# Stage two of a spectral block with its first products turned round: kf as weights, halves swapped by transfers, no second transposes

## The chip, the cores and the metric

One kernel runs on one core of a Trainium2 chip. The core has a matrix engine (PE, with its weight loads shown apart as PEld), a vector engine (DVE), an activation engine (ACT), a general engine (POOL) and a sync engine (SP) that here only issues transfers. Sixteen transfer engines (DMA) move data between the chip's main memory and the core's SBUF, whose 128 partitions the engines work on; PE writes into banks of PSUM, each of 128 partitions by 512 floats. The metric is the time of one execution on the device in microseconds, as the median of the runs.

## The reference: what is computed

```python
x = A_x                                    # [1, 2048, 512], float32
mod = (silu(c) @ w_mod).reshape(1, 6, 1, 512)
sa, ca, ga, sb, cb, gb = ...               # the six rows of mod
h = layernorm(x) * (1 + ca) + sa
X = rfft2(h, axes=(-2, -1)) * (w_r + 1j * w_i)      # w: [2048, 257]
x = x + ga * irfft2(X, s=(2048, 512))
h = layernorm(x) * (1 + cb) + sb
a = h @ w1 + b1                            # [2048, 1376]
x = x + gb * ((a * tanh(softplus(a))) @ w2)
```

A two-dimensional real Fourier transform of the normed input is multiplied, frequency by frequency, with a complex weight and transformed back. Then follow a second norm and a dense layer pair with the Mish function.

## The kernel before

The kernel has four stages, each with its order of work written out by hand (`manual_schedule`), so that on every engine and on every transfer queue instructions run in the order of the program text.

**Stage one** (to about 49 us) takes the 2048 rows as 128 x 16 and transforms along the 512 columns and along the 128. The result stands in `a_sb`, a tile [128, 64, 16, 8]: partition = one of 128 row frequencies, then 64 column frequencies `q`, 16 remaining rows `n`, and 8 entries (real and imaginary part of four column residues).

**Stage two** (the part that changes) does the remaining transform of length 16 x 4, the multiplication with the complex weight, and its inverse. It works on `groups` of four values of `q`, 512 columns wide: 17 groups, of which group 0 (`q` = 0) is special and has functions of its own (`z_in`, `z_mul`, `z_prod`, `z_back`, `z_out`). They are taken in the order `seq`. For a group five functions run:

- `p2_in` (L460): PE transposes the 128 x 128 blocks of `a_sb` of the group into a bank (L467), ACT copies it out (L470), and POOL adds a shift to one column per block (`p2_shift`, L478). Now the 128 lanes (16 x 4 x 2) stand on partitions.
- `p2_mul` (L480): four products (L488), with a block of the group as weights and the constant `kf` as moving data. That turns the block round again: the row frequencies stand on partitions, the lanes lie along the bank.
- `p2_prod` (L492): the complex multiplication. DVE makes two products of the bank with the real and with the imaginary weight (L504). Since real and imaginary lanes lie beside each other along the row, the sums of the crossed halves (L509, L510) are plain additions, on POOL except for five groups, whose first half DVE takes. The weight of a group is a tile of 256 KB; the first eight lie in `wqa`, the others in `wqb`, and all are loaded by SP's queue, before or at the start of the stage.
- `p2_back` (L513): PE transposes the result (L521), ACT copies it out (L524).
- `p2_out` (L527): four products with the constant `kv` (L534), and `store_d`, four ACT instructions that spread the bank over the tiles `d` (L387, L388).

A software pipeline runs these: eight `p2_in` ahead (`LEAD`), then the loop over steps `s`, where a step does `p2_prod` of group `s`, `p2_mul` of `s + 1`, `p2_in` of `s + 3`, `p2_back` of `s - 2` and `p2_out` of `s - 3`. Beside this, the steps hold the modulation columns: `mod_fetch` has SP load a 256 KB piece of `w_mod` two steps ahead into one of four buffers, and `mod_late` lets DVE multiply it with the silu row `scb` (in SBUF) and sum it up (L115). 16 such columns lie in steps 3 to 16. `flat` and `spread` write the gate out to memory and read it back to all partitions, on ACT's queue, `mod_gate` (L556) multiplies it into `kiv`, and the constants `kc` of stage three are loaded by SP in steps 13 and 15.

**Stage three** (L657 to L676) transforms back along 128 and 512 and adds to `x`. It needs all groups' `d`. **Stage four** is the dense pair. Both are dense on PE until the end.

PSUM has eight banks, two for each of the tags A, B, C and D: in stage two A takes `p2_in`, B `p2_mul`, C `p2_back`, D `p2_out`. Buffers with the tags g1, g2, y, t and h exist twice each.

Of the kernel before, what the change touches and what calls it, by code (L numbers as in the profile page):

```python
# [7 lines left out]
F32 = mybir.dt.float32  # L8
# [24 lines left out]
def tile_spectral_block(ctx: ExitStack, tc: tile.TileContext, x_d, w1_d, b1_d, w2_d,  # L33
# [54 lines left out]
    saz = base.tile([P, NQ], F32, name="saz")  # L88
    mraw = big.tile([P, N2, 256], F32, name="mraw", tag="da")
# [6 lines left out]
    wqa = pw.tile([P, 8, 2, 64, 4], F32, name="wqa")  # L96
# [17 lines left out]
    def mod_column(w, out, by, waste):  # L114
        nc.vector.scalar_tensor_tensor(waste, w, by, scb, op0=ALU.mult, op1=ALU.mult, accum_out=out)  # L115
# [70 lines left out]
    def load_rest():  # L186
        nc.sync.dma_start(kf, kf_d)
        nc.sync.dma_start(wz, wz_d)
        for i in range(8):
            nc.sync.dma_start(wqa[:, i], wq_d[i])  # L190
            if i == 2:
# [104 lines left out]
    with tc.manual_schedule():  # L296
# [16 lines left out]
        nc.vector.memset(eps, EPS)  # L313
        nc.vector.memset(b1n[:, NF - 1:NF], 0.0)
# [126 lines left out]
    def z_back():  # L441
        y = st.pop(("y", 0))
        pc = bank("C")
        nc.tensor.transpose(pc[:, 0:P], y[:, 0:P], ident)
        nc.tensor.transpose(pc[0:96, P:2 * P], y[:, 160:256], ident)
        t1, t2 = buf("t"), buf("t")
# [33 lines left out]
    def p2_mul(g):  # L480
        if g == 0:
            return z_mul()
        q0, nq = groups[g]
        w = nq * P
        z = st.pop(("z", g))
        pb = bank("B")
        for i in range(nq):
            nc.tensor.matmul(pb[:, 0:w].rearrange("p (e q) -> p e q", q=nq)[:, :, i], z[:, i * P:(i + 1) * P],  # L488
                             kf[:, 0:128], start=True, stop=True)
        st["pb", g] = pb  # L490

    def p2_prod(g):  # L492
        if g == 0:
            return z_prod()
        q0, nq = groups[g]
        w = nq * P
        pb = st.pop(("pb", g))
        pbv = pb[:, 0:w].rearrange("p (c j q) -> p c j q", q=nq, c=2)
        pr = []
        for i in range(2):  # L500
            t = buf(("g1", "g2")[i])
            tv = t[:, 0:w].rearrange("p (c j q) -> p c j q", q=nq, c=2)
            wt = (wqa, wqb)[q0 // 32][:, q0 // 4 % 8, i, :, q0 % 4:q0 % 4 + nq]
            nc.vector.tensor_tensor(tv, pbv, wt.unsqueeze(1).to_broadcast([P, 2, 64, nq]), op=ALU.mult)  # L504
            pr.append(t)
        y = buf("y")
        u = w // 2
        eng = nc.vector if g in (*seq[:3], *seq[-2:]) else nc.gpsimd
        eng.tensor_tensor(y[:, 0:u], pr[0][:, 0:u], pr[1][:, u:w], op=ALU.subtract)  # L509
        nc.gpsimd.tensor_tensor(y[:, u:w], pr[0][:, u:w], pr[1][:, 0:u], op=ALU.add)  # L510
        st["y", g] = y

    def p2_back(g):  # L513
        if g == 0:
            return z_back()
        q0, nq = groups[g]
        w = nq * P
        y = st.pop(("y", g))
        pc = bank("C")
        for i in range(nq):  # L520
            nc.tensor.transpose(pc[:, i * P:(i + 1) * P], y[:, 0:w].rearrange("p (e q) -> p e q", q=nq)[:, :, i],  # L521
                                ident)
        t = buf("t")
        nc.scalar.copy(t[:, 0:w], pc[:, 0:w])  # L524
        st["t", g] = t

    def p2_out(g):  # L527
# [3 lines left out]
        t = st.pop(("t", g))  # L531
        pd = bank("D")
        for i in range(nq):
            nc.tensor.matmul(pd[:, i * P:(i + 1) * P], t[:, i * P:(i + 1) * P], kv[:, 0:128],  # L534
# [4 lines left out]
    work_mod = {s: [] for s in range(len(seq) + 4)}  # L539
    when = (3, 4, 5, 6, 6, 7, 8, 9, 9, 10, 11, 12, 12, 13, 14, 16)  # L540
# [8 lines left out]
    def mod_late(s):  # L549
        for which, k in work_mod[s]:  # L550
            w = late.pop((which, k))
            mod_column(w, cols[:, 1, which - 1, k:k + 1] if which in (1, 2) else gcol[:, which // 3, k:k + 1], 1.0, w)
# [6 lines left out]
    wqb = pw.tile([P, 8, 2, 64, 4], F32, name="wqb", tag="half")  # L559
    with tc.manual_schedule():  # L560
        for i in range(8):
            nc.sync.dma_start(wqb[:, i], wq_d[8 + i])
        for i in range(LEAD):
# [4 lines left out]
            if i in (2, 4):  # L568
                p2_mul(seq[i // 2 - 1])
# [540 lines left out]
```

## Time and profile before

| | us |
|---|---|
| median of three runs | 392.35 |
| the three runs | 390.35, 392.35, 392.66 |
| the profiled execution | 390.15 |
| its span, first to last instruction | 388.2 |
| stage two, first transpose (L467) to first product of stage three (L663) | 49.42 to 97.55 |

| engine | busy us in the span | share |
|---|---|---|
| PE | 382.0 | 98% |
| DVE | 301.1 | 78% |
| ACT | 247.4 | 64% |
| POOL | 98.2 | 25% |

In the answers of the profile a group row reads: source line, engine, operation, output and inputs by their names in the program, shapes and count, then total busy time and the mean in ns, then idle time before it and who ended it. `buf` and `bank` are the names of all work buffers and banks. A timeline row begins with start and length in us. A product or transpose in the float type used here appears on PE as one entry for a transpose and two for a product. A transfer row has the size of one transfer and the median time from issue to landing. A row by stretches has start and end, length, busy time and instruction count for PE, PEld, DVE, ACT and POOL, the granted clock, the mean busy share of the transfer engines, and GB/s.

### The profile page before, as it was taken

The numbers are of one execution on the slowest core, as the hardware profiler recorded it, in microseconds if no ns is written. First come the engines' busy times: TensorE is split into PE (matmuls) and PEld (weight loads), VectorE is DVE, ScalarE is ACT, GpSimd is POOL, SyncE is SP. The second block draws the span as 40 slices with busy tenths as digits, with TensorE's granted clock in tenths as the row PEclk, the third lists the DMA queues.
The fourth block names the chain that finished last, engine by engine and source line by source line (L and its number), as shares of the span: only waits on it lengthen the run. The fifth ranks groups of instructions, "written<-read, shape, count | busy, mean of one in ns | idle before, by whom it ended". The sixth has DMA issues, their size and how long they took to land.

```text
span 388.2 us, 7440 instructions
## 1 busy us (share of the span) xinstructions
PE 382.0 (98%) x2769; PEld 356.3 (92%) x2769; DVE 301.1 (78%) x677; ACT 247.4 (64%) x545; POOL 98.2 (25%) x132
## 2 busy tenths in 40 slices
PE   8999999999999999999999999999999999999996
PEld 8999889999999998999998998999999999899985
DVE  2898978996399989888857866965966875987994
ACT  1798756778458638965845755664674674594751
POOL 0588637685166623300000000000000010017000
PEclk9999999999999999999999999999999999999999
DMA  7999994394052411200100100100100200113011
GB/s 270 354 320 380 296 357 114 95 292 160 26 155 77 143 49 28 57 2 0 56 0 3 54 2 0 57 0 2 55 2 0 76 0 2 48 57 115 2 56 54
DMA packets 21748, 36.98 MB, mean 95 GB/s; under 512 B 4016, under 2 KB 7184, under 8 KB 21456
## 3 DMA queue, kind: packets, MB, share of 16 engines
q1 hardware_dynamic: 20992, 35.85, 27.4%
q10 hardware_dynamic: 720, 0.66, 0.9%
q8 instruction: 22, 0.36, 0.4%
q14 instruction: 14, 0.11, 0.1%
HBM read 32.30 MB, written 4.20 MB: 94 GB/s over the span
## 4 chain that ended last, share of the span: by engine, by line
PE 89%; DVE 4%; ACT 3%; DMA 1%; issue 1%; SPq 1%; DVEq 0%; ACTq 0%
PE bank L805 24%; PE bank L752 20%; PE bank L754 10%; PE bank L208 4%; PE bank L488 4%; PE bank L534 3%; PE bank L673 3%; PE bank L253 3%; PE bank L663 3%; PE bank L664 3%; PE bank L797 2%; PE bank L818 2%; PE bank L642 2%; PE bank L467 2%; PE bank L521 1%; PE bank L255 1%
## 5 line engine op out<-in xcount | busy, mean ns | idle before, releaser
L762 ACT ACTIVATE buf<-bank,b1n 128x256 f32<-128x256 f32 (+1 forms) x88 | 40.8, 472 | 66.9 <-PE bank L754 66.5
L763 DVE TENSOR_TENSOR buf<-buf,bank 128x256 f32<-128x256 f32 (+1 forms) x88 | 35.3, 416 | 38.6 <-ACT buf L762 38.6
L715 DVE TENSOR_TENSOR al<-buf,ah 128x512 fp32r<-128x512 f32 (+2 forms) x85 | 53.5, 652 | 0.9 <-ACT ah L714 0.9
L734 POOL TENSOR_TENSOR buf<-buf,modr 128x512 f32<-128x512 f32 (+1 forms) x3 | 3.9, 1295 | 183.1 <-DVE buf L763 146.5
L752 PE MATMUL bank<-h2e,w1h 128*128 128x512 f32 (+1 forms) x176 | 48.5, 397 | 0.0
L752 PE MATMUL bank<-h2o,w1h 128*128 128x512 f32 (+1 forms) x176 | 48.3, 396 | 0.0
L714 ACT CAST ah<-buf 128x512 fp32r<-128x512 f32 (+2 forms) x85 | 43.0, 548 | 1.4 <-DVE buf L779 1.1
L779 DVE TENSOR_TENSOR buf<-buf 128x128 f32<-128x128 f32 x148 | 39.8, 310 | 3.5 <-ACT buf L769 2.2
L769 ACT ACTIVATE buf<-buf 128x512 f32<-128x512 f32 (+1 forms) x48 | 28.6, 596 | 14.7 <-DVE buf L763 14.6
L805 PE MATMUL bank<-w2a,ah 128*128 128x256 f32 x161 | 34.9, 286 | 0.0
L752 PEld LDWEIGHTS bank<-h2e,w1h 128*128 128x128 f32 (+1 forms) x176 | 30.1, 187 | 4.5
L752 PEld LDWEIGHTS bank<-h2o,w1h 128*128 128x128 f32 (+1 forms) x176 | 30.1, 187 | 4.4
L805 PE MATMUL bank<-w2b,ah 128*128 128x256 f32 x147 | 31.8, 283 | 0.0
L754 PEld LDWEIGHTS bank<-h2e,w1l 128*128 128x128 f32 (+1 forms) x176 | 26.7, 185 | 4.2
L754 PEld LDWEIGHTS bank<-h2o,w1l 128*128 128x128 f32 (+1 forms) x176 | 26.7, 185 | 4.2
L754 PE MATMUL bank<-h2e,w1l 128*128 128x256 f32 (+1 forms) x176 | 27.8, 280 | 0.0
L754 PE MATMUL bank<-h2o,w1l 128*128 128x256 f32 (+1 forms) x176 | 27.8, 280 | 0.0
L805 PEld LDWEIGHTS bank<-w2a,ah 128*128 128x128 f32 x161 | 26.7, 191 | 0.0
L663 PE MATMUL bank<-kc,d 128*128 128x128 f32 x128 | 24.8, 276 | 0.5 <-ACT d L387 0.5
L664 PE MATMUL bank<-kc,d 128*128 128x128 f32 x128 | 24.7, 275 | 0.0
L805 PEld LDWEIGHTS bank<-w2b,ah 128*128 128x128 f32 x147 | 24.6, 191 | 0.0
L122 DVE BATCH_NORM_STATS2 st<-x 128x6 f32<-128x512 f32 x32 | 22.0, 688 | 0.8 <-DMA x<-in_A_x_dram 0.4
(220 smaller groups left out, 1011.2 us busy)
## 6 DMA issues: line engine op xcount, KB each, us to landing
buf<-in_B_w_dram SPq DMA_DIRECT2D x20, 256.0 KB, 2.9
x<-in_A_x_dram SPq DMA_DIRECT2D x16, 256.0 KB, 5.1
xring<-in_x_t_dram SPq DMA_DIRECT2D x16, 256.0 KB, 5.0
wm<-in_w_mod_dram SPq DMA_DIRECT2D x16, 256.0 KB, 4.4
out_dram<-x SPq DMA_DIRECT2D x7, 512.0 KB, 2.6
mraw<-in_km_dram SPq DMA_DIRECT2D x16, 128.0 KB, 5.0
wqa<-in_w_q_dram SPq DMA_DIRECT2D x8, 256.0 KB, 4.4
wqb<-in_w_q_dram SPq DMA_DIRECT2D x8, 256.0 KB, 6.6
```

What stands on the lines that cost most here:

```text
L122: nc.vector.bn_stats(t, x[:, n, :])
L663: nc.tensor.matmul(o, dj[:, 0:128], kc[0][:, n, :], start=True, stop=False)
L664: nc.tensor.matmul(o, dj[:, 64:192], kc[1][:, n, :], start=False, stop=True)
L714: nc.scalar.copy(h, r)
L715: nc.vector.tensor_tensor(l, r, plain(h), op=ALU.subtract)
L752: nc.tensor.matmul(ps, w1h[:, k, fs], h[:, k], start=(k == 0), stop=False)
L754: nc.tensor.matmul(ps[:, 0:256], w1l[:, k, fs], h[:, k, 0], start=False, stop=(k == 3))
L762: nc.scalar.activation(o, ps[:, 256:], AF.Identity, bias=b1n[:rows, f:f + 1])
L763: nc.vector.tensor_tensor(o, o, ps[:, 0:256], op=ALU.add)
L769: nc.scalar.activation(o, o, AF.Mish)
L779: nc.vector.tensor_tensor(o, p, q, op=op)
L805: nc.tensor.matmul(o, a[p][:, e], w2[t][q][:, r], start=(own and half == 0 and t == 1 and i == 0), stop=(end and i == 2 and (n, half) != ( ...
```

## The change

The first product is turned round: in `p2_mul` `kf` is the weight and the whole group of 512 columns the moving data, so one product replaces four, and the lanes stay on partitions, real parts on 0 to 63 and imaginary parts on 64 to 127. The transposes of `p2_back` and ACT's copy after them are gone. In exchange the two halves that the complex product crosses now stand on different partitions. DVE multiplies the bank with a sign column `sgn` (+1 and -1) and the imaginary weight into `v`; two transfers on SP's queue copy the upper half of `v` to the lower half of `o` and the other way round; DVE multiplies the bank with the real weight straight into the group's place in `a_sb`; and two steps later POOL adds `o` there (`p2_add`, 512 wide). `p2_out` takes its weights from `a_sb`.

The weight now needs the same values on both halves of the partitions: a tile has 512 KB, `wqa` and `wqb` hold four each, and tiles are reused; SP loads the first eight, ACT's queue issues the other eight in the loop (`load_wq`). The freed C banks become a third bank for the first products (`spare`) and a copy of the silu row (`scp`) that `mod_late` reads. The loop starts at step 1 and its distances grow by one or two: `p2_mul` two steps ahead, `p2_in` four, `p2_add` two behind, `p2_out` five behind. The modulation columns spread over steps 3 to 21, `mod_gate` and the scale column move from step 14 to 16 and 18, and `kc` is loaded on ACT's queue in steps 12 and 13. Group 0 keeps its way, with its transposes into an A bank and its two buffers in a free tile of the early groups.

```diff
+    sgn = base.tile([P, 1], F32, name="sgn")
...
-    wqa = pw.tile([P, 8, 2, 64, 4], F32, name="wqa")
+    wqa = pw.tile([P, 4, 2, 512], F32, name="wqa")
...
-    def mod_column(w, out, by, waste):
-        nc.vector.scalar_tensor_tensor(waste, w, by, scb, op0=ALU.mult, op1=ALU.mult, accum_out=out)
+    def mod_column(w, out, by, waste, row=None):
+        nc.vector.scalar_tensor_tensor(waste, w, by, scb if row is None else row, op0=ALU.mult, op1=ALU.mult, accum_out=out)
...
-        for i in range(8):
+        for i in range(4):
             nc.sync.dma_start(wqa[:, i], wq_d[i])
-            if i == 2:
+            if i == 1:
...
+        nc.vector.memset(sgn[0:64], 1.0)
+        nc.vector.memset(sgn[64:128], -1.0)
...
-        pb = bank("B")
-        for i in range(nq):
-            nc.tensor.matmul(pb[:, 0:w].rearrange("p (e q) -> p e q", q=nq)[:, :, i], z[:, i * P:(i + 1) * P],
-                             kf[:, 0:128], start=True, stop=True)
+        pb = spare if seq.index(g) % 3 == 2 else bank("B")
+        nc.tensor.matmul(pb[:, 0:w], kf[:, 0:128], z[:, 0:w], start=True, stop=True)
         st["pb", g] = pb
+
+    scp, spare = bank("C"), bank("C")
+
+    def slot(g):
+        q0, nq = groups[g]
+        return a_sb[:, q0:q0 + nq].rearrange("p q n e -> p (q n e)")
+
+    def weights(g, i):
+        q0, nq = groups[g]
+        t = (wqa, wqb)[q0 // 16 % 2][:, q0 // 4 % 4, i]
+        return t[:, q0 % 4 * P:(q0 % 4 + nq) * P]
...
-        pbv = pb[:, 0:w].rearrange("p (c j q) -> p c j q", q=nq, c=2)
-        pr = []
-        for i in range(2):
-            t = buf(("g1", "g2")[i])
-            tv = t[:, 0:w].rearrange("p (c j q) -> p c j q", q=nq, c=2)
-            wt = (wqa, wqb)[q0 // 32][:, q0 // 4 % 8, i, :, q0 % 4:q0 % 4 + nq]
-            nc.vector.tensor_tensor(tv, pbv, wt.unsqueeze(1).to_broadcast([P, 2, 64, nq]), op=ALU.mult)
-            pr.append(t)
-        y = buf("y")
-        u = w // 2
-        eng = nc.vector if g in (*seq[:3], *seq[-2:]) else nc.gpsimd
-        eng.tensor_tensor(y[:, 0:u], pr[0][:, 0:u], pr[1][:, u:w], op=ALU.subtract)
-        nc.gpsimd.tensor_tensor(y[:, u:w], pr[0][:, u:w], pr[1][:, 0:u], op=ALU.add)
-        st["y", g] = y
-
-    def p2_back(g):
-        if g == 0:
-            return z_back()
...
+        v, o = (buf(t)[:, 0:w] for t in (("g1", "t"), ("g2", "y"))[seq.index(g) % 2])
+        nc.vector.scalar_tensor_tensor(v, pb[:, 0:w], sgn, weights(g, 1), op0=ALU.mult, op1=ALU.mult)
+        nc.sync.dma_start(o[0:64], v[64:128])
+        nc.sync.dma_start(o[64:128], v[0:64])
+        nc.vector.tensor_tensor(slot(g), pb[:, 0:w], weights(g, 0), op=ALU.mult)
+        st["o", g] = o
+
+    def p2_add(g):
+        if g:
+            nc.gpsimd.tensor_tensor(slot(g), slot(g), st.pop(("o", g)), op=ALU.add)
...
-    when = (3, 4, 5, 6, 6, 7, 8, 9, 9, 10, 11, 12, 12, 13, 14, 16)
+    when = (3, 4, 5, 6, 8, 9, 11, 12, 14, 15, 16, 17, 18, 19, 20, 21)
...
+    def load_wq(i):
+        nc.scalar.dma_start((wqa, wqb)[i // 4 % 2][:, i % 4], wq_d[i])
+
     with tc.manual_schedule():
-        for i in range(8):
-            nc.sync.dma_start(wqb[:, i], wq_d[8 + i])
+        nc.scalar.copy(scp, scb)
+        for i in range(4, 8):
+            nc.sync.dma_start(wqb[:, i % 4], wq_d[i])
...
-        for s in range(len(seq) + 3):
+        for s in range(1, len(seq) + 5):
             mod_fetch(s + 2)
-            if 0 < s < len(seq):
+            if 4 <= s < len(seq) + 2 and seq[s - 2] and groups[seq[s - 2]][0] < 32:
+                load_wq(groups[seq[s - 2]][0] // 4 + 8)
+            if s == 2:
+                load_wq(8)
+            if s == 3:
+                load_wq(9)
+            if 0 <= s - 2 < len(seq):
+                p2_add(seq[s - 2])
+            if 2 <= s < len(seq):
                 p2_prod(seq[s])
-            if 2 <= s + 1 < len(seq):
-                p2_mul(seq[s + 1])
-            if LEAD <= s + 3 < len(seq):
-                p2_in(seq[s + 3])
+            if 4 <= s + 2 < len(seq):
+                p2_mul(seq[s + 2])
+            if LEAD <= s + 4 < len(seq):
+                p2_in(seq[s + 4])
             mod_late(s)
-            if 2 <= s < len(seq) + 2:
-                p2_back(seq[s - 2])
-            if s >= 3:
-                p2_out(seq[s - 3])
+            if s == 6:
+                z_back()
+            if s >= 5:
+                p2_out(seq[s - 5])
...
-            if s == 14:
+            if s == 16:
                 mod_gate()
-            if s == 14:
+            if s == 18:
                 plus_one(cols[:, 1, 1, :], cols[:, 1, 1, :])
-            if s in (13, 15):
-                for i, t in (((0, "cr"),) if s == 13 else ((1, "ci"),)):
+            if s in (12, 13):
+                for i, t in (((0, "cr"),) if s == 12 else ((1, "ci"),)):
                     kc.append(big.tile([P, N2, P], F32, name=f"kc{i}", tag=t))
-                    nc.sync.dma_start(kc[i], kc_d[:, i, :, :])
+                    nc.scalar.dma_start(kc[i], kc_d[:, i, :, :])
...
-    wq = wq.reshape(2, 128, 4, 16, 16, 4).transpose(4, 1, 0, 2, 3, 5).reshape(16, 128, 2, 64, 4)
+    wq = wq.reshape(2, 128, 64, 16, 4).transpose(3, 2, 0, 4, 1).reshape(16, 64, 2, 512)
+    wq = np.concatenate([wq, wq], 1)
```

35 lines of the change are left out of this document (12 added, 23 removed).

## The prediction

> **What bounds the kernel now.** I read the page first (span and chain of waits), then busy time by stretch, then the weight-load timeline of one step, the groups of stage two, and the transfers.
>
> ```profile
> span 388.2 us, 7440 instructions
> ...
> PE 89%; DVE 4%; ACT 3%; DMA 1%; issue 1%; SPq 1%; DVEq 0%; ACTq 0%
> ```
>
> The profiled execution took 390.15 us, so 1.95 us lie outside the span. The chain that ended last is 89% PE, so the first question is where stage two stands in it. Busy time by stretch (length; PE, PEld, DVE, ACT, POOL busy; clock, transfer share, GB/s) answers that: the first row is stage two, from its first transpose to the first product of stage three, the second is stage three.
>
> ```profile
> 49.42:97.55 48.13, 46.83 (x397) 44.65 (x396) 39.26 (x79) 33.59 (x103) 30.16 (x50) 1.00 0.62 202
> 97.55:140.90 43.35, 43.10 (x383) 42.91 (x384) 36.27 (x67) 27.28 (x57) 23.40 (x24) 1.00 0.33 97
> ```
>
> PE is busy 46.83 of 48.13 us, and stage three is equally full, so a shorter stage two moves everything behind it forward. The transfer engines stand at 0.62 and 202 GB/s. One steady step, as PE loads its weights (start, length):
>
> ```profile
> 79.36 0.47 PEld L467 LDWEIGHTS bank<-ident,a_sb 128*128 128x128 f32 x4
> 79.80 0.56 PEld L521 LDWEIGHTS bank<-ident,buf 128*128 128x128 f32 x4
> 80.27 0.98 PEld L534 LDWEIGHTS bank<-kv,buf 128*128 128x128 f32 x8
> 81.17 0.97 PEld L488 LDWEIGHTS bank<-kf,buf 128*128 128x128 f32 x8
> 82.06 0.47 PEld L467 LDWEIGHTS bank<-ident,a_sb 128*128 128x128 f32 x4
> ```
>
> Start to start: first transposes 0.44, second transposes 0.47, last products 0.90, first products 0.89, in all 2.70 us a step without a gap. PE sets the pace. The other engines' groups in stage two:
>
> ```profile
> L115 DVE SCALAR_TENSOR_TENSOR wm<-wm,modr 128x512 f32<-128x512 f32 x16 | 14.0, 888 | 0.0
> L510 POOL TENSOR_TENSOR buf<-buf 128x256 f32<-128x256 f32 x15 | 13.8, 920 | 2.1 <-DVE buf L504 1.6 <-PE bank L521 0.5
> L387 ACT COPY d<-bank 128x256 f32<-128x256 f32 x29 | 11.0, 380 | 2.9 <-PE bank L534 2.9
> L504 DVE TENSOR_TENSOR buf<-bank,wqb 128x512 f32<-128x512 f32 x16 | 10.2, 678 | 0.6 <-POOL buf L510 0.6
> L521 PE MATMUL bank<-ident,buf 128*128 128x128 f32 x63 | 10.1, 283 | 0.0
> L524 ACT COPY buf<-bank 128x512 f32<-128x512 f32 x15 | 9.0, 601 | 3.0 <-PE bank L521 3.0
> L388 ACT ACTIVATE d<-bank 128x128 f32<-128x128 f32 x29 | 8.7, 300 | 0.0
> L509 POOL TENSOR_TENSOR buf<-buf 128x256 f32<-128x256 f32 x11 | 8.4, 765 | 7.5 <-POOL buf L478 2.8 <-PE bank L521 2.6 <-PE bank L409 2.1
> L478 POOL TENSOR_TENSOR buf<-buf,saz 128x4 f32<-128x4 f32 x9 | 5.4, 603 | 0.0
> L470 ACT COPY buf<-bank 128x512 f32<-128x512 f32 x9 | 5.3, 590 | 3.0 <-PE bank L467 2.6 <-POOL buf L478 0.4
> L115 DVE DVE_READ_ACCUMULATOR wm<-wm,modr 128x1 f32 x16 | 1.2, 77 | 0.0
> ```
>
> ACT needs 0.59 + 0.60 + 2 x 0.38 + 2 x 0.30 = 2.55 us a step, POOL 0.77 + 0.92 + 0.60 = 2.29, DVE 2 x 0.68 + 0.89 + 0.08 = 2.33 in a step with a modulation column. All are just under PE's 2.70.
>
> **What the change does to PE.** The 63 second transposes (x63, L521) go: 63/4 x 0.47 = 7.4 us. Special group 0 keeps its own two. The four first products of a group become one with kf as weights and 512 moving columns. Of such a width in this type no row exists; the nearest are products of 128 and 160 columns:
>
> ```profile
> L409 PE MATMUL bank<-kf,early x2: 299/351/403, 58.3 to 58.5; 128*128 128x160 f32 x2
> L409 PE MATMUL bank<-kv,buf x2: 273/274/275, 70.0 to 70.1; 128*128 128x128 f32 x2
> ```
>
> Shortest against shortest, 32 columns cost 26 ns, so 512 cost 0.42 us; two entries a product give 0.83 us against 0.89. By the medians 32 columns cost 77 ns, and it would be dearer by far (2 x 1.2 us); but at that price four narrow ones would not fit into their 0.89 us, so I take the shortest: 0.06 x 15.75, about 0.9 us at best, 0.5 us taken. PE's path is then 7.9 us shorter, 2.2 us a step, and stage three would start at 97.55 - 7.9 = 89.65.
>
> **ACT, DVE and POOL.** Now each has to fit 2.2 us. ACT loses L524: 1.95 us. It gains the copy of the silu row to a bank, 0.59 us like its other 512-wide copies, at the stage's start; this row shows the gap that covers it:
>
> ```profile
> 50.01 1.02 ACT L470 COPY early<-bank 128x384 f32<-128x384 f32 x2 [0.64 <-PE bank L467]
> ```
>
> DVE's first product takes a sign column as well. A row of the same operation with a bank and a column, POOL's only wide sums, and DVE's columns with a bank in them stand here:
>
> ```profile
> L223 DVE SCALAR_TENSOR_TENSOR bank<-modr,mv,bank x16: 722/725/752, 11.1 to 45.1; 128x512 f32<-128x512 f32 x16
> L237 POOL TENSOR_TENSOR buf<-buf x7: 1274/1284/1675, 15.9 to 42.9; 128x512 fp32r<-128x512 f32 x7
> L115 DVE SCALAR_TENSOR_TENSOR bank<-wms,modr x4: 673/682/692, 40.1 to 46.4; 128x512 f32<-128x512 f32 x4
> ```
>
> DVE: 0.73 + 0.68, and 0.68 to 0.89 + 0.08 for a column, so 2.17 to 2.38 us in a step with a column and 1.41 without; 11 of the steps 3 to 16 have one, which averages under 2.2. Its half additions of five groups leave it. POOL: one 512-wide sum of 1.28 to 1.68 for 0.77 + 0.92, plus the shift, at most 0.60: 1.9 to 2.3. I take 1.9, since DVE's products read a bank and no longer meet it with two SBUF inputs. None of the three becomes the bound. The sign column's memsets fall into DVE's first wait for data and cost nothing; gate and scale columns, moved two and four steps later, are used only in stage three.
>
> **The swaps.** Each group now waits for two SBUF-to-SBUF transfers of 64 partitions, 128 KB each. No row shows such a one. Issue to landing in the trace:
>
> ```profile
> wm<-in_w_mod_dram SPq DMA_DIRECT2D x16, 256.0 KB, 4.4
> wqb<-in_w_q_dram SPq DMA_DIRECT2D x8, 256.0 KB, 6.6
> kc<-in_kc_dram SPq DMA_DIRECT2D x2, 1024.0 KB, 8.2
> out_dram<-x ACTq DMA_DIRECT2D x1, 128.0 KB, 1.8
> ```
>
> So 1.8 us (128 KB, nothing else moving) to 6.6 (full engines); I take 4.4, that of the columns that share SP's queue. POOL's addition waits for it, and behind it on POOL stands the shift of the group six places on, which PE multiplies four steps after the swap's own: 4 x 2.2 = 8.8 less 0.73 (first product), 1.68 and 0.60 leaves 5.8 us. The result itself is due five steps on, which is later. At 4.4 all is covered; at 6.6 some 0.8 us a step shows. On SP the swaps stand behind a column's fetch and ahead of the next one, which DVE uses three steps later; each fits.
>
> **The transfers as a whole** are the term that I think decides. A weight tile is now stored once per half: 512 KB for 256 KB. ACT can ask for the first of the eight late tiles when its early copies are done, and the loop's steps begin when the early products are:
>
> ```profile
> 51.90 1.02 DVE L504 TENSOR_TENSOR buf<-bank,wqa 128x384 f32<-128x384 f32 x2 [0.20 <-PE bank L488]
> 54.91 1.95 PE L488 MATMUL bank<-kf,early 128*128 128x128 f32 x16
> 55.11 0.59 ACT L470 COPY early<-bank 128x512 f32<-128x512 f32 x1 [0.26 <-PE bank L467]
> ```
>
> That is between 55.7 and 56.9; I take 56.5. From there until stage three can start there must move: eight weight tiles (4.19 MB), 13 columns (3.41), 14 swap pairs (3.67), kc (2.10), the spread gate (0.26), in all 13.63 MB. The four tiles before (2.1 MB) and the rest of the first four replace what moves there now. Full engines in the trace:
>
> ```profile
> 46.00:56.50 10.50, 10.17 (x81) 9.20 (x81) 7.71 (x17) 5.87 (x12) 3.24 (x12) 1.00 1.00 361
> 48.00:56.00 8.00, 7.68 (x66) 7.09 (x65) 5.27 (x12) 4.61 (x9) 2.45 (x11) 1.00 1.03 375
> 84.00:88.00 4.00, 4.00 (x38) 4.00 (x37) 4.00 (x8) 3.07 (x10) 3.33 (x6) 1.00 1.02 413
> ```
>
> At 375 GB/s (2 KB rows, as the swaps have) 13.63 MB take 36.3 us and end at 92.8; at 413 (kc's long rows) 33.0 us, ending at 89.5. I take 375, because most of the bytes are in short rows. 92.8 is later than PE's 89.65, so the transfers set the end: 4.75 us are won of PE's 7.9. The last group's own tail fits below that: from its first product at 51.9 (above) DVE needs about 31.5 us (15.75 x 1.41 + 11 x 0.76 + 1 for group 0), 83.4, then swap 4.4, sum 1.3, product 0.9, ACT 0.68: 90.7.
>
> **Rivals.** *PE's pace holds (first).* Weight tiles are asked for six steps ahead, and the 84 to 88 row shows 413. Then 7.9 us are won: 382.3. Against it: it needs 13.63 MB in 33 us, with no pause.
>
> *The swaps run at half rate (second; slower).* All transfers in the rows above reach 128 partitions; one that reaches 64 may move at half their rate, 187 GB/s, so each swap byte counts double. Place: the 14 swap pairs. Price: 9.96 + 2 x 3.67 = 17.3 MB, 46.1 us, stage three at 102.6, 5.05 us late: 395.2. It decides from a factor f with (9.96 + 3.67 f)/0.375 = 41.05 us, which is f = 1.48. For it: no row shows a half-height transfer at full rate. Against it: two queues are served at once, so the ports that one half leaves idle can take weight bytes. The Trainium skill has the rule for this: its page "SBUF — State Buffer", section "Door 1: The DMA port swizzle", says that partitions 0 to 63 reach 8 of 16 ports and gives 196 GB/s measured against 328 for 128 partitions. By those figures f would be 1.67 and an estimate for the start of stage three 99.4 us, 392.0 in all; no run here shows it yet.
>
> *The middle (third).* Either f near 1.3 to 1.5 (stage three at 95.8 to 97.6), or held queues. The waits of SP show the latter's mechanism: a column's fetch waited for weight tiles that it shares no buffer with.
>
> ```profile
> SPq L547 <- DMA wqb<-in_w_q_dram: 2.2, 5, 0.9
> ```
>
> Weight loads are now issued by ACT, ahead of its copies and stores; if one waits so for the transfer eight issues before it (the fetches came behind eight tiles; here that is two steps, 4.4 us, against 6.6 to land), ACT stands still up to 2 us, and its spare time is 0.25 us a step. Either way 2 to 5 us of the forecast's gain go: 387.4 to 390.4. That the transposes don't go is excluded by the code.
>
> **Numbers.** Forecast 390.15 - 4.75 = 385.4. The profiled execution is 2.2 us below the median 392.35 and 0.2 below the fastest of the three runs, 390.35; the result will be a median too, so I add half the distance: 386.5. Chances: forecast 0.32, PE's pace 0.25, the middle 0.30, half rate 0.13. A measurement of this kernel tells about 1% (3.9 us) from no change. Faster: 0.25 and four fifths of the forecast, 0.51; slower: 0.13; same: the middle and the rest, 0.36. The range runs from PE's pace, 382.3, past the slow end of the middle to an f of 1.6 (98.7, that is 391.3) with the runs' whole 2.2 us on top, 393.5; above that lies most of the half rate. The forecast's own range, at 361 to 413 GB/s (94.3 to 89.65) and 0 to 2.2 on top, is 382.3 to 389.1.
>
> **What would show it.** Right: no second transposes, a step of 2.2 to 2.5 us on PE, transfer share near 1.0 and 370 GB/s or more from 57 us on, stage three's first product at 91 to 94. Swaps landing in under 5.8 us and POOL's sum at 1.3 us confirm the cover. Wrong: the transfer share near 1 with the rate below 330 GB/s in stretches with swaps (half rate); ACT idle ahead of copies with its queue at a load (held); a share well under 1 and PE without gaps (first rival); or the 512-wide product at over 1 us.

## Result, and the profile after

The changed kernel took 409.09 us (median of four runs, 408.06 to 410.04); the kernel before, run beside it, 391.55 (390.35 to 392.66). The ratio is 1.047, with a 95% interval of 1.0444 to 1.0495: **4.7% slower**. The forecast was 386.5 with a range to 393.5, so sign and range were both missed. The profiled execution took 408.47 us.

The page of the changed kernel, its span and its chain of waits:

```profile
span 406.7 us, 7147 instructions
...
PE 75%; DMA 13%; issue 4%; DVE 3%; ACT 2%; POOL 2%; SPq 1%; POOLq 0%; ACTq 0%; DVEq 0%
```

PE held 89% of the chain before; now transfers hold 13% of it. Where, the stretches show (start and end, length; PE, PEld, DVE, ACT, POOL busy; clock, transfer share, GB/s):

```profile
49.00:57.00 8.00, 7.87 (x49) 5.60 (x48) 6.12 (x12) 4.65 (x10) 1.81 (x10) 1.00 0.86 301
57.00:108.00 51.00, 34.96 (x184) 26.02 (x184) 26.49 (x55) 19.34 (x72) 20.06 (x29) 0.86 0.96 271
113.70:158.40 44.70, 43.71 (x374) 43.52 (x375) 34.70 (x66) 26.93 (x55) 23.52 (x24) 0.96 0.33 92
```

Up to 57 us PE is full as before. From there to 108 it is busy for 35 of 51 us, while the transfer engines stand at 0.96 and move only 271 GB/s. Stage three's first kind of product, with its first and last start, before and after:

```profile
L663 PE MATMUL bank<-kc,d x128: 275/275/377, 97.6 to 139.8; 128*128 128x128 f32 x128
```

```profile
L669 PE MATMUL bank<-kc,d x128: 274/275/582, 113.7 to 158.4; 128*128 128x128 f32 x128
```

The stage begins 16.1 us later, and these products run over 44.7 us instead of 42.2, at a granted clock of 0.96 where the stage had 1.00 before. So of the 18.3 us between the two profiled executions, 16 arise ahead of stage three and about the rest in it.

PE's own steps did get shorter. Its weight loads in a stretch in which it need not wait (start, length):

```profile
74.47 0.97 PEld L527 LDWEIGHTS bank<-kv,a_sb 128*128 128x128 f32 x8
75.36 0.30 PEld L490 LDWEIGHTS bank<-buf,kf 128*128 128x128 f32 x2
...
76.34 0.36 PEld L470 LDWEIGHTS bank<-ident,a_sb 128*128 128x128 f32 x3 [0.29 <-issue]
76.66 0.97 PEld L527 LDWEIGHTS bank<-kv,a_sb 128*128 128x128 f32 x8
```

From 74.47 to 76.66 are 2.19 us, where the kernel before took 2.70. The groups of the engines beside it, as priced:

```profile
L518 POOL TENSOR_TENSOR a_sb<-a_sb,buf 128x512 f32<-128x512 f32 (+1 forms) x16 | 20.2, 1263 | 23.6 <-DMA buf<-buf 21.5 <-DVE a_sb L513 2.0
L390 ACT COPY d<-bank 128x256 f32<-128x256 f32 (+2 forms) x34 | 12.6, 375 | 12.5 <-PE bank L527 7.1 <-DMA buf<-buf 5.4
L116 DVE SCALAR_TENSOR_TENSOR wm<-wm,bank 128x512 f32<-128x512 f32 x16 | 10.9, 686 | 18.6 <-DMA wm<-in_w_mod_dram 18.6
L510 DVE SCALAR_TENSOR_TENSOR buf<-bank,sgn,wqb 128x512 f32<-128x512 f32 x8 | 6.0, 747 | 5.6 <-POOL buf L439 5.6
```

Their durations are as forecast (1.26, 0.38, 0.69, 0.75 us). What is new is the idle time behind the bars: POOL waits 21.5 us for swaps, DVE 18.6 for columns, ACT 5.4 with an issue of its own that waits for a swap to land. The chain of waits of the changed kernel between 57 and 109 us, its transfers (start, length):

```profile
57.37 7.83 DMA buf<-buf
...
76.86 6.88 DMA wm<-in_w_mod_dram
...
83.82 6.15 DMA wqb<-in_w_q_dram
...
90.55 8.75 DMA buf<-buf
99.29 0.02 issue
99.31 8.34 DMA buf<-buf
```

From 76.86 us on, one landing is followed by the next issue, and each of these transfers takes 6 to 9 us to land. Four single stretches, and the one ahead of stage three, show what that does to PE:

```profile
61.00:65.00 4.00, 1.36 (x11) 1.08 (x9) 0.70 (x2) 0.59 (x2) 0.00 (x0) 1.00 1.03 342
65.00:69.00 4.00, 0.17 (x1) 0.20 (x2) 1.67 (x3) 0.74 (x4) 3.52 (x7) 0.63 0.83 261
97.00:101.00 4.00, 2.97 (x14) 3.00 (x15) 0.82 (x2) 2.71 (x12) 1.26 (x1) 0.50 1.06 276
105.00:109.00 4.00, 0.21 (x2) 0.01 (x1) 0.99 (x3) 1.18 (x5) 1.19 (x1) 0.75 1.06 240
109.10:113.30 4.20, 4.12 (x16) 3.56 (x16) 2.33 (x8) 1.01 (x5) 1.27 (x1) 0.50 0.90 325
```

PE works for 1.5 of the 8 us from 61 on and for 0.2 of the 4 from 105 on. The clock is down to 0.50 to 0.75 in the last four rows, so what is due then takes longer too: the last products of two groups, sixteen entries, take 4.12 us in the last row, where the kernel before needed 0.90 for the eight of one group.

### The profile page after: what moved, and what is told of

The parts are those of the page before. It is cut to its first block, busy times and chain, and to the rows that moved or that the text cites. A ratio compares the mean times of both kernels' runs of the same rounds, so it can differ in the third digit from the quotient of the medians.

```text
span 406.7 us, 7147 instructions
## 1 busy us (share of the span) xinstructions
PE 382.9 (94%) x2612; PEld 347.3 (85%) x2612; DVE 297.5 (73%) x674; ACT 240.0 (59%) x530; POOL 92.7 (23%) x121
## 4 chain that ended last, share of the span: by engine, by line
PE 75%; DMA 13%; issue 4%; DVE 3%; ACT 2%; POOL 2%; SPq 1%; POOLq 0%; ACTq 0%; DVEq 0%
PE bank L811 23%; PE bank L758 19%; PE bank L760 10%; DMA buf<-buf 6%; PE bank L209 3%; PE bank L254 2%; PE bank L803 2%; PE bank L679 2%; DMA buf<-in_B_w_dram 2%; PE bank L824 2%; PE bank L669 2%; PE bank L670 2%; PE bank L648 2%; DMA wm<-in_w_mod_dram 2%; DMA wqb<-in_w_q_dram 2%
## 5 line engine op out<-in xcount | busy, mean ns | idle before, releaser
L721 DVE TENSOR_TENSOR al<-buf,ah 128x512 fp32r<-128x512 f32 (+2 forms) x85 | 52.2, 636 | 0.8 <-ACT ah L720 0.8
L785 DVE TENSOR_TENSOR buf<-buf 128x128 f32<-128x128 f32 x148 | 42.0, 325 | 3.5 <-ACT buf L775 2.2
L527 PE MATMUL bank<-kv,a_sb 128*128 128x128 f32 x126 | 21.6, 331 | 9.0 <-issue 4.6
L527 PEld LDWEIGHTS bank<-kv,a_sb 128*128 128x128 f32 x126 | 19.9, 241 | 11.0 <-issue 5.4
L669 PE MATMUL bank<-kc,d 128*128 128x128 f32 x128 | 25.9, 285 | 0.5 <-ACT d L390 0.5
L670 PE MATMUL bank<-kc,d 128*128 128x128 f32 x128 | 25.7, 284 | 0.0
```

Of the source, the lines that this page charges most:

```text
L527: nc.tensor.matmul(pd[:, i * P:(i + 1) * P], y[:, i * P:(i + 1) * P], kv[:, 0:128], start=True, stop=True)
L669: nc.tensor.matmul(o, dj[:, 0:128], kc[0][:, n, :], start=True, stop=False)
L670: nc.tensor.matmul(o, dj[:, 64:192], kc[1][:, n, :], start=False, stop=True)
L721: nc.vector.tensor_tensor(l, r, plain(h), op=ALU.subtract)
L785: nc.vector.tensor_tensor(o, p, q, op=op)
```

## Experiments

Unless said otherwise each is an edit of the changed kernel, and its time is that of one execution, to be held against the 408.47 of the changed kernel's. The kernel before, run beside them, had medians of 389.8 to 392.5, so differences under some 2 us are not read.

### The swaps taken away, and their form

Without any transfer (POOL adds `v` itself, so the crossing is left out):

```diff
-        nc.sync.dma_start(o[0:64], v[64:128])
-        nc.sync.dma_start(o[64:128], v[0:64])
...
-        st["o", g] = o
+        st["o", g] = v
```

> No transfers between the halves at all: POOL adds the sign-weighted product uncrossed, so the crossing is left out; the doubled weights and the order stay. 'Half height': PE's pace is left, stage three starts at 90 to 92, time 382 to 386. 'Order' (bursts of weight tiles on ACT's queue, the columns behind them): 392 to 400. 'Bytes': 400 or more.

Measured 385.83 us. Its first products of stage three, and the stretch that goes with them:

```profile
L667 PE MATMUL bank<-kc,d x128: 275/275/377, 90.5 to 133.9; 128*128 128x128 f32 x128
```

```profile
57.00:90.00 33.00, 31.85 (x201) 24.04 (x200) 27.80 (x58) 20.84 (x77) 22.80 (x30) 1.00 0.92 310
```

PE is full at clock 1.00 and stage three begins at 90.5, where the forecast had PE's own path at 89.65. So the arithmetic of PE, DVE, ACT and POOL was right, the doubled weight tiles fit in beside it at 0.92 of the engines, and the swaps alone cost 23 us (408.47 - 385.83; by the start of stage three 113.7 - 90.5).

Two transfers per group that reach all 128 partitions, each over half the columns:

```diff
-        nc.sync.dma_start(o[0:64], v[64:128])
-        nc.sync.dma_start(o[64:128], v[0:64])
+        nc.sync.dma_start(o[:, 0:w // 2], v[:, 0:w // 2])
+        nc.sync.dma_start(o[:, w // 2:w], v[:, w // 2:w])
```

> The two transfers of a group carry the same bytes but run over all 128 partitions, half of the columns each, from a partition to itself; the halves are not crossed, so that part of the complex product is left out. The changed kernel took 408.5 us in its profiled execution, stage three started at 113.9, and the transfer engines were busy 0.96 at 271 GB/s from 57 to 108 us. Theory 'half height' (a transfer that reaches 64 partitions moves at half rate or less): the rate rises to 350 GB/s or more, stage three starts at 92 to 99, time 387 to 394. Theory 'order' (issues wait for earlier landings, ACT and POOL stand behind them, whatever the transfers' shape): within 3 us of the changed kernel, 405 to 411. Theory 'bytes' (the doubled weights alone fill the engines): the same, 405 to 411.

Measured 405.3 us, stage three at 111.8: 3 us only. The number of transfers is the same here, and their rows are 1 KB long instead of 2. Half-height without the crossing (`o[0:64]` from `v[0:64]`, `o[64:128]` from `v[64:128]`):

> Two transfers of 64 partitions as in the changed kernel, but each from a partition to itself; the crossing of the halves is left out. 'Half height': no change against the changed kernel, 405 to 411. If it is the way from one half to the other that costs: 387 to 395. 'Order' and 'bytes': 405 to 411.

408.17 us: it makes no difference that the halves cross. One transfer of 256 KB over 128 partitions per group:

```diff
+        nc.sync.dma_start(o, v)
```

> One transfer of 256 KB over all 128 partitions in place of the two of a group, each partition to itself (the halves are not crossed): the bytes of the first experiment in rows of 2 KB instead of 1 KB, in half as many transfers. That one took 405.3. Theory 'eight in flight' (an issue on either queue waits for the landing of the transfer eight before it; with four transfers a step and 6 to 7 us to land, a step cannot take less than about 3.3 us): a step has 3 transfers instead of 4, stage three starts 10 us or more earlier, 392 to 397. Theory 'engine time' (copies inside SBUF hold the transfer engines): 2 KB rows help a little, 400 to 405.

397.41 us, stage three at 104.8. Same bytes, all partitions, half the number: 11 of the 23 us. Against the two full-height transfers, 8 of them come from making one of two (with rows of 2 KB for 1 KB).

### What the transfers can carry by themselves

The kernel before, with runs of transfers between tiles appended to its end, one kind after the other, nothing else moving: half-height crossed pairs of 128 KB, full-height in 1 KB rows, full-height in 2 KB rows, loads from main memory, and at last 24 half-height ones on SP's queue beside six loads of 512 KB on ACT's.

```diff
+    for i in range(12):
+        cross(i)
...
+        nc.sync.dma_start(pa[:, i], x[:, i])
...
+        nc.sync.dma_start(pa[:, i], xv[:, i])
...
+    for i in range(12):
+        cross(i)
+        if i % 2 == 0:
+            nc.scalar.dma_start(pb[:, i:i + 2], xv[:, i:i + 2])
```

> The kernel before, and behind its last result five runs of transfers with nothing else on the chip, each after the landing of the one before: 24 swaps of 64 partitions crossed (128 KB, 2 KB rows), 24 copies of 128 partitions (128 KB, 1 KB rows), 12 copies of 128 partitions (256 KB, 2 KB rows), 12 loads from memory (256 KB, 2 KB rows), and 24 swaps with 6 loads of 512 KB beside them on ACT's queue. 'Half height': the first run moves at half the rate of the third, some 190 against 375 GB/s. 'Engine time': all copies are well under the loads. 'Eight in flight' says nothing on rates; the landing of a transfer in a full run is then eight times its share.

Its stretches, in that order (the last two numbers are transfer share and GB/s), and the landing of the 128 KB swaps, alone in the first run and beside loads in the last:

```profile
390.00:404.00 14.00, 0.00 (x0) 0.00 (x0) 0.00 (x0) 0.00 (x0) 0.00 (x0) 0.58 0.87 202
408.00:420.00 12.00, 0.00 (x0) 0.00 (x0) 0.00 (x0) 0.00 (x0) 0.00 (x0) 0.50 0.61 206
424.00:430.00 6.00, 0.00 (x0) 0.00 (x0) 0.00 (x0) 0.00 (x0) 0.00 (x0) 0.50 1.03 382
434.00:442.00 8.00, 0.00 (x0) 0.00 (x0) 0.00 (x0) 0.00 (x0) 0.00 (x0) 0.50 0.98 343
444.50:468.70 24.20, 0.00 (x0) 0.00 (x0) 0.02 (x1) 0.00 (x0) 0.00 (x0) 0.50 0.94 260
```

```profile
pa<-x SPq DMA_DIRECT2D x24, 128.0 KB, 2.3
pa<-x SPq DMA_DIRECT2D x24, 128.0 KB, 5.1
```

GB/s over share gives the rate of a fully busy set of engines. For the first two runs this is an estimate, since SP issued one of these transfers every 0.64 us and the engines were not full. The rates are: 202/0.87 = 232 for the half-height swaps, 382/1.03 = 371 for the full-height copies of 2 KB rows, 206/0.61 = 338 for 1 KB rows, 343/0.98 = 350 for loads. The rival's factor f is 371/232 = 1.60, above the 1.48 from which it decides. The Trainium skill's page "SBUF — State Buffer", section "Door 1: The DMA port swizzle", has 196 against 328 GB/s, a factor of 1.67; the factor of these rows, 1.60, comes near it. The last stretch answers what the forecast leaned on: 3.15 MB of swaps take 13.6 us at 232, 3.15 MB of loads 9.0 at 350, together 22.6, and the engines were busy for 0.94 x 24.2 = 22.7. The times add up: in this mix the loads of the other queue did not fill what the swaps leave unused. The Trainium skill's page "DMA: Bandwidth & Descriptors", section "Back-pressure in remote DMA", says that stalled writes hold up an engine's other queues too; it says so of transfers between cores. Added times within one core would fit that, but no run here shows whether writes stall.

### The loads beside the swaps

Only the real half of each weight tile is loaded and used for both products:

```diff
-        nc.scalar.dma_start((wqa, wqb)[i // 4 % 2][:, i % 4], wq_d[i])
+        nc.scalar.dma_start((wqa, wqb)[i // 4 % 2][:, i % 4, 0], wq_d[i, :, 0])
```

> Each weight tile loads its real half only (256 KB instead of 512) and that half is used for both products; the imaginary weight is left out; swaps as in the changed kernel. 2.1 MB less move after 56.5 us. 'Half height': at the 271 GB/s of the changed kernel that is 7.7 us, 399 to 402. 'Bytes': the engines have room again and the time is 392 or less. 'Order' (the issue of the weight tiles is as before, only their landing is shorter): 402 to 407.

403.0 us, stage three at 109.2 (the imaginary weight is left out). So beside the swaps the weights' doubling costs 5.5 us. Loads in pairs (half as many, twice the size):

```diff
+                nc.sync.dma_start(w, wm_d[2 + which, k:k + 2].rearrange("k p f -> p k f"))
...
+            nc.scalar.dma_start((wqa, wqb)[i // 4 % 2][:, i % 4 - 1:i % 4 + 1],
+                                wq_d[i - 1:i + 1].rearrange("a p c f -> p a c f"))
```

> The changed kernel, complete, same bytes and same swaps, but the weight tiles 4 to 15 and the modulation columns are loaded in pairs: 14 transfers fewer in the stage (6 for 12 tiles, 8 for 16 columns). 'Eight in flight': 14 of some 65 transfers less, stage three 8 to 14 us earlier, 395 to 401. 'Engine time': no change, 406 to 410.

406.09 us, stage three at 113.9 as before: the number of loads is not it. So the theory 'eight in flight', which had 395 to 401 here, falls, though the one copy per group had come near its 392 to 397. One copy per group and half the weights together:

> The two earlier edits together: one copy of 256 KB over 128 partitions per group (the crossing is left out) and only the real half of the weight tiles from HBM (the imaginary weight is left out). If the transfer engines' time sets the stretch, the sum from 57 us is 3.93 MB at 371 GB/s, 10.6 us, 9.4 MB of loads at 350, 26.9 us, and some 5 us of holes: stage three at 98 to 101, 391 to 394 us. If the delay of each transfer sets it, halving the loads changes little from the 104.8 and 397.4 of the one copy alone: 103 to 105, 395 to 397.

398.84 us, no faster than the one copy alone (397.41), though 2 MB less had to move. Stage three begins at 103.6 instead of 104.8 and gives that back behind, at a clock of 0.96. Engine time as the whole story had 391 to 394 and falls here.

### The queues

Weight tiles and `kc` issued on POOL's queue instead of ACT's:

```diff
-        nc.scalar.dma_start((wqa, wqb)[i // 4 % 2][:, i % 4], wq_d[i])
+        nc.gpsimd.dma_start((wqa, wqb)[i // 4 % 2][:, i % 4], wq_d[i])
...
-                    nc.scalar.dma_start(kc[i], kc_d[:, i, :, :])
+                    nc.gpsimd.dma_start(kc[i], kc_d[:, i, :, :])
```

> The changed kernel, complete, with one thing moved: the weight tiles from the eighth on and both kc transfers are issued on POOL's queue instead of ACT's, so that ACT's copies stand behind no issue that waits for a landing. Theory A (the transfers' engine time sets the stretch, the holds only show it): share and rate between 57 and 108 us stay at 0.95 to 1.0 and 265 to 285 GB/s, stage three's first product at 112 to 115, 404 to 409 us. Theory B (half of the loss is ACT held behind its load issues, which leaves PE idle and its clock low): first product at 101 to 108, 395 to 403 us. Sign of the mechanism: ACT's idle time ahead of its loads and copies that a transfer ends (12.7 us in the changed kernel) falls under 3 us; if it does and the time stays, theory B falls. POOL's own sums may then stand behind the issues instead, which would cost less because one POOL step is 1.9 us of 2.7.

408.73 us. ACT's long waits behind its own issues are gone (it now idles for PE), and the time stays. The same with the one copy per group:

> One copy of 256 KB over 128 partitions per group in place of the two half-height swaps (the crossing of the halves is left out, so the output is not the reference's), and the loads on POOL's queue as in the run before. With the loads on ACT's queue the one copy took 397.4 us, its first stage-three product stood at 104.8, and ACT was held 7.6 us at the second kc issue. If that hold was worth its length, the first product comes at 96 to 99 and the time is 388 to 392; if the transfers would have been late anyway, 102 to 105 and 395 to 398. Without any transfer for the swaps it was 385.8 and 90.6, which is the floor.

397.19 us beside 397.41. In the run with ACT's queue the hold had looked decisive. Its order of work there (start, length, and in brackets the idle time before and what ended it):

```profile
94.08 2.51 POOL L517 TENSOR_TENSOR a_sb<-a_sb,buf 128x512 f32<-128x512 f32 x2 [3.32 <-DMA buf<-buf]
...
94.92 0.37 ACT L390 COPY d<-bank 128x256 f32<-128x256 f32 x1 [7.59 <-DMA wm<-in_w_mod_dram]
...
96.01 8.17 PE L526 MATMUL bank<-kv,a_sb 128*128 128x128 f32 x47 [7.48 <-POOL a_sb L517]
```

ACT's stores stand 7.6 us behind an issue that waits for an earlier load. But PE waits for POOL's sum, which waits for its swap and ends at 95.4: at the same place the swap is late by itself, and only the last 0.6 us of PE's wait can be ACT's, so taking the hold away wins nothing that is read here.

SP's queue was held as well. Its longest wait of this kind between 57 and 104 us (in all, times, longest), in the run with ACT's queue and in the run with POOL's:

```profile
SPq L511 <- DMA buf<-buf: 8.6, 3, 4.6
```

```profile
SPq L539 <- DMA buf<-buf: 2.0, 2, 1.2
```

In all, SP's swaps and column fetches waited there for earlier landings for 13.8 us with ACT's queue and for 2.3 with POOL's. The time is the same, so these holds do not make it either. (With two half-height swaps they are 20.5 us with ACT's queue and 19.4 with POOL's, so there the same was not tested.)

Group 0's products in buffers of their own, since DVE waited 5.6 us at 61 to 67 for POOL to free them:

```diff
-            t = buf(("g1", "g2")[i])
+            t = early[0][:, 1 + i]
...
-        y = buf("y")
+        y = early[0][:, 3]
```

> The changed kernel, complete, with buffers of its own for group 0's products, so that DVE's product of the sixth group need not wait for POOL's work on group 0, which stands behind an addition that waits for a swap (DVE waited 5.6 us there). If that hold decides: 5 us less, 402 to 404. 'Eight in flight' and 'engine time': the transfers set the pace later anyway, 406 to 409.

406.92 us; DVE's wait at L510 falls from 5.6 to 1.5 us, stage three still begins at 113.7. And POOL's sum one step later, so that a late swap holds up the next group's shift less:

```diff
-            if 0 <= s - 2 < len(seq):
-                p2_add(seq[s - 2])
+            if 0 <= s - 3 < len(seq):
+                p2_add(seq[s - 3])
```

> The changed kernel, complete, with POOL's sum of each group one step later, so that a late swap has 2.7 us more before POOL waits for it with the next group's shift (and so PE's kf product) behind. If POOL's queue carries the swaps' delay to PE, stage three comes 4 to 10 us earlier, 398 to 404 us; if the transfers' rate sets it, 406 to 410 us.

405.61 us, stage three at 111.4: 3 us, a time between the two ranges named and under the 4 to 10 that this coupling would have been worth.

### Bytes or transfers

The swaps cut to half their columns (POOL adds the same half twice), and to 32 columns:

```diff
+        nc.sync.dma_start(o[0:64, 0:w // 2], v[64:128, 0:w // 2])
+        nc.sync.dma_start(o[64:128, 0:w // 2], v[0:64, 0:w // 2])
```

> The changed kernel with the two half-height, crossed transfers of each group cut to half their columns, 64 KB each; POOL adds the same half twice, so its work, the chain and the count of transfers stay (half of the crossed product is left out). If engine time sets the stretch, the swaps' 16.9 us fall to 8.5: stage three at 101 to 105, 394 to 399 us. If the number of transfers or the delay of each sets it, stage three stays at 110 to 114, 404 to 409 us.

> The changed kernel with the two transfers of each group cut to 32 columns, 8 KB each, and POOL adding those columns throughout (15 sixteenths of the crossed product are left out): the count, issues and waits stay and the bytes go. If the swaps' engine time is the loss, stage three comes at 92 to 97, 387 to 392 us. If a swap of any size costs as much as the half-size run leaves over (a line through 408.5 and 402.8), 396 to 399 us with stage three near 103.

402.80 and 396.54 us. With 128, 64 and 8 KB a transfer the three times are 408.47, 402.80 and 396.54: nearly a straight line, 12 us for the bytes. But it does not end at 385.83: a swap of 8 KB still costs 10.7 us over none. (The rows get shorter with the transfers, 2 KB, 1 KB and 128 bytes; what that alone does was not measured.) In the kernel with 8 KB swaps its transfers between 56 and 104 us, then the first of them in the chain of waits, then PE's two gaps:

```profile
buf<-buf SPq DMA_DIRECT2D x29, 8.0 KB, 3.9
```

```profile
57.76 5.23 DMA buf<-buf
```

```profile
61.00:65.00 4.00, 1.71 (x12) 1.22 (x10) 0.70 (x2) 1.91 (x6) 1.85 (x3) 1.00 1.09 352
65.00:69.00 4.00, 2.43 (x9) 1.85 (x10) 3.81 (x8) 0.27 (x1) 1.84 (x5) 0.80 0.36 138
...
89.00:93.00 4.00, 1.16 (x8) 0.97 (x8) 3.08 (x5) 0.08 (x1) 2.17 (x2) 0.79 0.87 326
93.00:97.00 4.00, 2.34 (x11) 2.37 (x12) 2.09 (x6) 2.14 (x9) 2.50 (x2) 0.50 1.02 328
```

In the probe 128 KB landed in 2.3 us without loads and in 5.1 beside them; here 8 KB take 3.9 at the median and 5.23 where two weight tiles had just been asked for. In the four stretches PE is idle for 8.4 us of 16 and its clock falls to 0.50. The same with the loads on POOL's queue:

> The run before with the weight tiles and kc issued on POOL's queue. If what the small swaps still cost is the wait of an issue on ACT's or SP's queue for the landing of an earlier transfer of the other's, this comes 4 us or more under the run before; if not, within 1.5 us of it.

396.69 us, no change again, though the waits of SP's swaps and fetches for earlier landings fell from 7.5 to 3.4 us as well. So the 10.7 us that remain at 8 KB are shown, and that neither the bulk of the bytes nor ACT's holds make them, nor SP's as far as these runs removed them. The likeliest cause left is the long landing among the loads, with PE's gaps and low clock behind it; no run took that away by itself, so it is argued and stays open.

### The halves crossed by the engines

If transfers are the loss, engines with room can cross the halves. In seven groups POOL copies the two halves across, in six ACT (the expectation has these two numbers the other way round), in three DVE writes its product crossed:

```diff
+    WAYS = "PAPDPAPAPDPAPAPAD"
...
-        nc.sync.dma_start(o[0:64], v[64:128])
-        nc.sync.dma_start(o[64:128], v[0:64])
+            for a, b in HALF:
+                if how == "A":
+                    nc.scalar.copy(o[a], v[b])
+                else:
+                    nc.gpsimd.tensor_copy(o[a], v[b])
```

> Complete: the changed kernel without the transfers for the swaps; the halves are crossed by the engines, group by group in a fixed pattern: in six groups POOL copies the two halves across partitions, in seven ACT does so one step later, in three DVE writes its product crossed in two half-height instructions. If the transfers were the whole loss and the engines have the room that the profile shows (ACT 1.95, DVE 1.4 to 2.4, POOL 1.9 of 2.7 us per step), stage three starts at 91 to 95 and the time is 386 to 390, 0.5 to 1.5% under the kernel before. If a half-height instruction costs as much as a full-height one and the crossing group's engine becomes the bound (POOL 1.28 + 2 x 1.28 in its steps), stage three starts at 96 to 101, 391 to 397.

388.96 us (median of ten), 0.9963 of the kernel before (95% interval 0.9939 to 0.9986). Stage three begins at 94.9, PE's clock stays at 1.00. From 57 to 95 us the crossing copies and the sum:

```profile
L537 POOL TENSOR_TENSOR a_sb<-a_sb,buf 128x512 f32<-128x512 f32 x15 | 19.8, 1331 | 0.5
L531 ACT COPY buf<-buf 64x512 f32<-64x512 f32 x12 | 7.4, 617 | 1.8 <-POOL a_sb L537 1.6
L533 POOL COPY buf<-buf 64x512 f32<-64x512 f32 x12 | 7.3, 608 | 0.6
```

A copy of 64 partitions takes 0.61 us, so a crossing is 1.2 us. POOL needs 1.33 + 1.2 in its groups, more than PE's 2.2; that is the likely place of the 4 us against 90.5, but no run took it away. With the last two groups' sums on DVE and the gate's product behind them:

> Complete: the kernel with the halves crossed by the engines, with the last two groups' sums on DVE instead of POOL, and the gate's product on DVE moved behind them. In the kernel without it POOL made three sums in a row from 88.6 to 93.2 and PE waited 3.3 us for them; with two of them on DVE (0.69 us each in place of 1.27) stage three should start at 92 to 93 in place of 94.9, and the time be 386 to 388, 0.7 to 1.2% under the kernel before. If DVE, which then has the modulation columns behind these sums, is late with the column factors instead, the gain is given back in stage three: 388 to 390.

388.54 us, 0.9952 (0.9927 to 0.9976), stage three at 94.8: the expected 2 us did not come. PE now waits for POOL's crossing and sum of the third last group instead, and behind it for ACT's stores. With the modulation columns earlier as well:

> Complete: the version before, with the modulation columns taken one to three steps earlier, so that the gate's row is spread earlier on POOL and the first split of w1 stands behind it for less time (PE idled 1.4 us near 113 us for it). If that is so, 385 to 387; if DVE then falls behind PE's pace in stage two, 388 to 391.

387.98 us, 0.9935 (0.9913 to 0.9958). It was to close a gap of PE in stage three; that stretch in the version before, and in this one:

```profile
110.00:120.00 10.00, 8.64 (x78) 8.45 (x77) 8.03 (x18) 7.48 (x14) 4.57 (x5) 1.00 0.46 130
```

```profile
110.00:120.00 10.00, 9.81 (x88) 9.62 (x87) 9.66 (x18) 8.15 (x16) 5.82 (x6) 1.00 0.45 131
```

The gap closed (8.64 to 9.81 of 10 us). The time is above the 385 to 387 expected, and the intervals of the three versions overlap; that this last one is under the kernel before is measured, that it is under the two others is not. None reaches the 1% from which the prediction called a kernel faster.

## Why the prediction was wrong, point by point

**PE's removed work: right.** Step 2.19 us against 2.2 forecast; without the swaps stage three came at 90.5 against 89.65, so the first rival's 382.3 was what the engines alone would nearly have given (385.8 measured, of which 3.3 lie outside the span of 382.5, where the profiled execution of before had 1.95).

**ACT, DVE, POOL: right.** The durations held to 0.03 us; none became the bound.

**Weights through the engines: nearly right.** 0.92 of the engines at 310 GB/s carry them without the swaps.

**"At 375 GB/s 13.63 MB take 36.3 us": the step that failed first.** The sign named for it was seen: a share of 0.96 with 271 GB/s, under the 330. The bytes were sized about rightly: 51 us at 271 are 13.8 MB. By the rates measured alone the swaps take 3.67/0.232 = 15.8 us, not 9.8, and the other 9.96 MB 28.5 at 350, not 26.6. That is an estimate of 44.3 us and puts stage three at 100.8, 8 us later than forecast, and already later than in the kernel before. I took 375 from a stretch of full-height loads and carried it over to half-height transfers of which no row existed. In the kernel itself, full-height swaps won 3 us (405.3, in 1 KB rows) and taking nearly all their bytes away 12 (396.54).

**"At 4.4 all is covered": the step that failed second.** The swaps landed in 6.4 us at the median and 7.8 to 8.8 on the chain. I had bounded the landing by 6.6, the longest median of short transfers before. A median is no bound, and a landing depends on what else moves: 2.3 us without loads and 5.1 beside them in the probe. Over a slack of 5.8 I had priced an excess at 0.8 us a step, as if PE went on at a lower pace. Instead PE stood for 4 us and more at a time and restarted at half clock; even 8 KB swaps cost 10.7 us. How these 10.7 us come about stays open.

**"The last group's own tail: 90.7".** DVE's last product was not the start of it: the last swap on the chain landed at 107.65, and from there to stage three passed 6 us, where one sum, one product and ACT had been put at 2.9. Two groups were still due: two sums of 1.27 us, and their products at a clock of 0.50.

**Rivals.** The half rate shows in the probe (f = 1.60), and the reason given against it, that the idle ports can take weight bytes, did not hold in the mixed stretch. But its price (391.3 at this f) is 5.9 us over the forecast, a quarter of the 23 that the swaps cost, and a chance of 0.13 was too small for a term without a row. Issues held by an earlier landing exist, up to 7.6 us long on ACT's queue (with one copy per group) and not 2, yet where runs removed them the time stayed. No rival had the swaps costing something whatever their size; that was not thought of.

## What to carry to other kernels

A transfer put into a chain of dependent steps had two prices here, one that went with its bytes (12 us) and one that stayed at 8 KB (10.7 us). Neither could be read from the kernel before, in which the transfer engines had room (a share of 0.62 in stage two). Where an operation has no row in the trace, the range has to take in the worst rival at its full amount: here 395.2, which would have covered "slower", though not the 409.09 measured. And a long wait in the profile is not yet a cost: the 7.6 us hold of ACT was worth nothing, and only the run without it showed that.

## What was unexpected of the hardware

Transfers between tiles that reach 64 of 128 partitions moved 232 GB/s with the engines fully busy (an estimate from 202 at a share of 0.87), against 371 for 128 partitions, and loads of another queue did not fill the rest (260 GB/s mixed, times additive). A transfer of 8 KB took 3.9 us to land among loads; one of 128 KB took 2.3 without loads and 5.1 beside them. A copy over 64 partitions and 512 columns costs ACT 0.62 us and POOL 0.61; ACT's copies of a bank over 128 partitions take 0.59.
